# Sliding-window attention and an ELU layer on one core: first loads reordered, two score steps moved, the last step split

## The chip, the core and the metric

The kernel runs on one core of one Trainium2 chip, in one launch. The metric is the device time of that core in microseconds (us), lower is better. Before the change it is 311.78 us, the median of 8 runs (311.09 to 313.75). One run was taken with the hardware profiler; every line quoted from a page, a timeline or a DMA view is from such an execution.

## The reference

q, k and v are fp32 of shape (8 batches, 8 heads, 576 tokens, 64). The attention looks 32 tokens to each side; its result, with the heads side by side, is the input of a two-layer block with an ELU between the layers.

```python
scores = (q @ k.T) / sqrt(64)             # per batch and head
scores = where(|i - j| <= 32, scores, -1e9)
attn   = exp(scores - max) ; attn /= sum + 1e-9
x      = (attn @ v) as (4608 tokens, 512)
h      = x @ w_in                          # (512, 2048)
g      = where(h > 0, h, exp(min(h, 0)) - 1)
out    = g @ w_out                         # (2048, 512) -> (4608, 512) fp32
```

## The kernel before, in words

**Attention by pairs.** The 576 tokens of a batch are 9 query blocks of 64; two blocks make a pair, and there are 36 pairs. For a pair, `scores` (L279, PE, 16 matmuls) multiplies 128 keys by 64 queries per head into two PSUM banks, `exponential` (L290, ACT) writes them to SBUF, `mask` (L299, DVE) zeroes what lies outside the window, `pv` (L311, PE, 16 matmuls) multiplies by the values with a column of ones, `normalize` (L320 and L323, DVE) divides, `x_transpose` (L332, PE) turns the result and `x_evac` (L345, a copy on the engine named) puts it into `xT`. `V_e` holds the values in tiles of 128 tokens that start 32 tokens early; `V_o` is the same shifted by 64, made by `rotate_v` (L136, DVE) from two neighbouring tiles. `edges(i)` clears the borders of value buffer i and sets its ones.

**q and k.** `load_qk` (L115) loads one half of the tokens of a batch (`HALF_A`: tokens 0 to 287, `HALF_B`: 288 to 575) or all, in two transfers of 288 KB for the two heads of each couple (576 KB for all the tokens). `cast_qk` makes bf16 of them, `transpose_qk` (L262, PE) transposes, and a copy on ACT or DVE puts the result into `qT` or `kT`. Pairs 0 and 1 need only the first half of batch 0, pairs 2 and 3 its second half. Values and weights are loaded by POOL (L129, L150, L157) with a cast to bf16, on one queue in the order of issue; `load_w_in(c)` and `load_w_out(c)` bring a quarter each ("slice c"), enough for two of the eight steps of a tile. SP and ACT have queues of their own (q1 and q10 in the profile; POOL's is q0).

**The two layers by steps.** A tile t is 256 tokens, two pairs; there are 18. A step is a tile and a group s of 256 of the 2048 hidden units, so 144 steps in all. `mm1(kk)` (L540, 8 matmuls) makes the first product of step kk in one PSUM bank (tags h0 and h1 in turn), then ACT takes the exponential (L546) and DVE subtracts one (L548); `elu(kk)` (L553, DVE) takes max and min; `mm2(kk)` (L568, 4 matmuls) adds the second product into the two banks `psY` of the tile. Tiles 0 and 1 take turns: steps 0 to 3 are tile 0 with slices 0 and 1, steps 4 to 7 tile 1 with the same slices, so the values of pairs 2 and 3 are needed from step 4 on. When a tile is complete its two banks are copied to SBUF and written by SP; in the last tile each bank is copied in halves, by ACT and DVE, and written from the ACT and SP queues.

**What sets the order.** The schedule is written out by hand: each engine executes in program order, and a tile's dependencies add the waits. Before the loop there is a front (L376 to L407): casts, transposes, scores and the rest of pairs 0 and 1, with `idle(n, tag)` matmuls on zeros (L370) between them. In the loop (L591) the slots of step kk come in the order "first", `elu(kk-1)`, "dve", `mm1(kk)`, "mid", `mm2`, "end", and `at(kk, slot, ...)` puts work into one. A table gives the `mm2` of the first steps: `{1: (0,), 2: (1,), 3: (2,), 4: ()}`; after it, `mm2(kk-2)` belongs to step kk. A `gate` (L143) is a transfer of one element: it makes SP wait until what it reads is there, and so holds what SP issues behind it. One waits for `w_out` slice 0, and behind it stand batch 1's first q and k loads.

Of the kernel before, what the change touches and what calls it, by code (L numbers as in the profile page):

```python
# [9 lines left out]
FP32 = mybir.dt.float32  # L10
BF16 = mybir.dt.bfloat16
# [10 lines left out]
def kernel(  # L22
# [9 lines left out]
    nc = tc.nc  # L32
# [81 lines left out]

    def load_qk(b, which, part, eng=nc.sync):  # L115
        z, nj = part
        t = lpool.tile([128, 2, nj * D], FP32, tag=f"f{which}{nj}",
                       name=f"f{which}")
        qk_f[b, which, z] = t
        src = (q, k)[which][b, :, z * NC * nj:(z + 1) * NC * nj, :].rearrange(  # L120
            "(g h) (c j) d -> c g h (j d)", h=2, j=nj)
        for h in range(2):
            eng.dma_start(out=t[:, h, :], in_=src[:, :, h, :])

    def load_v(b, m):
# [5 lines left out]
            in_=v[b, :, lo + p0:lo + p1, :].rearrange("h p d -> p h d"))  # L131

    def rotate_v(b, m0, m1, parts=(0, 1)):
        e, o = V_e[b % 3], V_o[b % 3]
        for z in parts:
            nc.vector.tensor_copy(o[64 * z:64 * (z + 1), m0:m1],  # L136
                                  e[64 * (1 - z):64 * (2 - z),
                                    m0 + z:m1 + z])

    gate_t = cpool.tile([1, 8], BF16, name="gate_t")  # L140
    gates = [0]

    def gate(src):  # L143
        n = gates[0]
        gates[0] += 1
        nc.sync.dma_start(out=gate_t[:, n:n + 1], in_=src)

# [16 lines left out]

    for part in (HALF_A, HALF_B):
        load_qk(0, 0, part)
        load_qk(0, 1, part, nc.scalar)

# [3 lines left out]
    def edges(i):  # L172
# [22 lines left out]
        out=masks, in_=masks, compare_op=ALU.is_ge, fill=0.0,  # L195
        base=2 * WIN, pattern=[[0, 5], [1, QB]], channel_multiplier=-1)
    for mi in (0, 4):
        nc.gpsimd.affine_select(
            out=masks[:, mi, :], in_=masks[:, mi, :], compare_op=ALU.is_ge,
            fill=0.0, base=-WIN, pattern=[[0, QB]], channel_multiplier=1)  # L200
# [5 lines left out]

    for m in (1, 0, 2, 3, 4):
        load_v(0, m)
# [166 lines left out]

    idle(10, "y1")  # L376
    front_cast(0, HALF_A, nc.vector)
    front_transpose(0, HALF_A, nc.scalar, ("h0", "h1"))
    idle(2, "u")
    front_cast(1, HALF_A, nc.vector)  # L380
    for (j0, n), tag, eng in zip(SPLIT, ("y0", "y1"), (nc.scalar, nc.vector)):
        transpose_qk(0, 1, HALF_A, j0, n, eng, tag)
    for i, tag in ((0, "s"), (1, "u")):
        scores(i, tag)
        exponential(i)
    idle(2, "y0")
    front_cast(0, HALF_B, nc.vector)
    front_transpose(0, HALF_B, nc.scalar, ("h0", "h1"))
    mask(0)
    cast_qk(0, 1, HALF_B, *SPLIT[0], nc.vector)  # L390
    mask(1)
    cast_qk(0, 1, HALF_B, *SPLIT[1], nc.vector)
    idle(6, "y1")
    front_transpose(1, HALF_B, nc.scalar, ("y0", "y1"))
    rotate_v(0, 0, 2)
    for i in (0, 1):
        pv(i)
    for i in (0, 1):
        normalize(i)
    edges(2)  # L400
    rotate_v(0, 2, VS - 1)
    idle(4, "h0")
    for i in (0, 1):
        x_transpose(i)
    for i in (0, 1):
        x_evac(i, nc.scalar)
    idle(5, "h1")  # L407

    gate(w_out_sb[0:1, NFO // 4 - 1, D_MODEL - 1:D_MODEL])
    for which in range(2):  # L410
        load_qk(1, which, HALF_A)
    for c in range(2, 4):
        load_w_in(c)
        load_w_out(c)
        if c == 2:
            for m in range(3):
                load_v(1, m)
    gate(w_in_at(3))
# [28 lines left out]
    for i, tag in ((2, "s"), (3, "u")):  # L447
        at(0, "mid", scores, i, tag)
        at(0, "mid", exponential, i)
        at(1, "dve", mask, i)  # L450
        at(1, "end", pv, i)
        at(2, "dve", normalize, i)
        at(3, "mid", x_transpose, i)
    at(3, "mid", x_evac, 2, nc.scalar)
    at(3, "mid", x_evac, 3, nc.vector)
    at(4, "dve", swap_pools)

    for part, kq in ((HALF_A, 7), (HALF_B, 15)):
        for which in range(2):
            at(kq - 1 + which, "mid", cast_qk, 1, which, part, 0, SJ // 2,  # L460
               (nc.scalar, nc.vector)[which])
            at(kq + which, "mid", transpose_qk, 1, which, part, 0, SJ // 2,
               nc.scalar, "s")
    for m in range(VS):
        at(16 + m, "mid", load_v, 2, m)
# [66 lines left out]
    def mm1(kk):  # L532
        t, s = order[kk]
        h = kk % 2
        ps = ps_tile([128, FG, TT], FP32, f"h{h}", "ps")
        psH[kk] = ps
        for j in range(FG):
            fo = s * FG + j
            for do in range(NDO):
                nc.tensor.matmul(  # L540
                    ps[:, j, :],
                    lhsT=w_in_sb[:, do, fo * 128:(fo + 1) * 128],
                    rhs=xT[t][:, :, do, :],
                    start=(do == 0), stop=(do == NDO - 1))
        e_sb = mpool.tile([128, FG, TT], FP32, tag="e_sb")
        nc.scalar.activation(e_sb, ps, AX.Exp)  # L546
        m_sb = mpool.tile([128, FG, TT], BF16, tag="m_sb")
        nc.vector.tensor_scalar(m_sb, e_sb, -1.0, None, ALU.add)  # L548
        m_t[kk] = m_sb

    def elu(kk):
        g_sb = mpool.tile([128, FG, TT], BF16, tag="g_sb")
        nc.vector.scalar_tensor_tensor(  # L553
            g_sb, psH.pop(kk), 0.0, m_t.pop(kk), ALU.max, ALU.min)
        g_t[kk] = g_sb

    out_t = out.rearrange("(t ts p) c -> t p ts c", p=128, ts=TT // 128)

    def mm2(kk):
# [6 lines left out]
        for ts in range(2):  # L566
            for j in range(FG):
# [5 lines left out]
                    stop=(s == STEPS - 1 and j == FG - 1))  # L573
            if last:

                half = D_MODEL // 2
                for c, eng in enumerate((nc.scalar, nc.vector)):
                    y_sb = opool.tile([128, half], FP32, tag=f"y_last{c}",
                                      name="y_last")
                    copy_on(eng, y_sb, psY[t][ts][:, c * half:(c + 1) * half])  # L580
                    (nc.scalar, nc.sync)[c].dma_start(
                        out_t[t, :, ts, c * half:(c + 1) * half], y_sb)
        if s == STEPS - 1 and not last:
            for ts, eng in enumerate((nc.scalar, nc.vector)):
                y_sb = opool.tile([128, D_MODEL], FP32, tag=f"y_sb{ts}",
                                  name="y_sb")
                copy_on(eng, y_sb, psY[t][ts])
                nc.sync.dma_start(out_t[t, :, ts, :], y_sb)

    LAG = 2  # L590
    for kk in range(NSTEP + LAG):  # L591
        run(kk, "first")
        if 1 <= kk <= NSTEP:
            elu(kk - 1)
# [4 lines left out]

        for n in {1: (0,), 2: (1,), 3: (2,), 4: ()}.get(  # L600
                kk, (kk - LAG,) if kk >= LAG else ()):
            mm2(n)
# [31 lines left out]
```

The softmax here doesn't subtract the row's maximum and nothing guards it: scores larger than these inputs give would overflow.

## Time and profile before

| | |
|---|---|
| median of 8 runs | 311.78 us |
| the profiled execution's own time | 311.12 us |
| its span in the trace | 309.4 us |
| PE, DVE, ACT, POOL busy | 293.5, 247.0, 169.9, 43.1 us |
| step 0's first product starts | 18.15 us |
| last first product (step 143) ends, by the chain | 301.9 us |
| last matmul ends | 304.9 us |
| read from and written to HBM | 36.70 MB, 15.34 MB |

A timeline line has: start and duration in us, the engine, the line of the kernel, the operation, what it writes "<-" what it reads, the shape, and how many instructions were merged (x8); in brackets stands how long the engine was idle before and what ended that. PEld is PE's weight load, SPq and ACTq the instructions that issue transfers. A DMA view's queue line has packets, MB written and the share of the 16 DMA engines. The granted TensorE clock of the whole span is 0.995.

### The profile page before, as it was taken

Reading aid. Unit: us, or ns where it says so; the run is one execution under the profiler, and the core shown is the slowest. Engines: PE = TensorE matmul, PEld = TensorE weight load, DVE = VectorE, ACT = ScalarE, POOL = GpSimd, SP = SyncE. Lnnn points to the kernel's source line nnn. Section 1 sums busy time; section 2 is a strip of 40 time slices with the busy share of each in tenths; the row PEclk is TensorE's granted clock in tenths of the full one; section 3 lists DMA queues with packets and bytes.
Section 4 is the critical chain, followed back from the end, with each engine's and each line's share of the span. In section 5 each row is a group of like instructions: output and inputs, shape, how many; then the busy total and the mean of one; then the engine's idle time right before and its main releaser. Section 6 shows DMA issues by size and latency. Waiting matters only on the chain.

```text
span 309.4 us, 7519 instructions
## 1 busy us (share of the span) xinstructions
PE 293.5 (95%) x3003; PEld 197.2 (64%) x3057; DVE 247.0 (80%) x479; ACT 169.9 (55%) x255; POOL 43.1 (14%) x60
## 2 busy tenths in 40 slices
PE   6789998999999999999999999999999999999993
PEld 2456666577665666666666666666666666666661
DVE  5787687899979788888888888888888787877663
ACT  2753755777664674667366736663535354543431
POOL 8632542040111202020202000000000000000000
PEclk9999999999999999999999999999999999999998
DMA  6999999999979899599999999388111111111012
GB/s 240 193 207 270 189 162 364 373 229 289 245 171 196 309 244 197 148 154 255 240 159 202 301 238 196 110 166 169 70 36 70 34 70 35 70 34 70 24 46 69
DMA packets 91943, 52.93 MB, mean 171 GB/s; under 512 B 76548, under 2 KB 81156, under 8 KB 91908
## 3 DMA queue, kind: packets, MB, share of 16 engines
q1 hardware_dynamic: 47876, 36.19, 45.6%
q0 software_dynamic: 41728, 8.92, 39.0%
q10 hardware_dynamic: 2304, 7.34, 7.0%
q8 instruction: 24, 0.39, 0.5%
q14 instruction: 11, 0.09, 0.1%
HBM read 36.70 MB, written 15.34 MB: 168 GB/s over the span
## 4 chain that ended last, share of the span: by engine, by line
PE 76%; DVE 11%; DMA 6%; issue 3%; ACT 3%; ACTq 0%; SPq 0%; DVEq 0%
PE ps L540 35%; PE psY L568 33%; DMA Ve<-in_v_dram 5%; PE psS L311 3%; DVE g_sb L553 3%; PE psS L279 3%; DVE m_sb L548 2%; DVE pm L299 2%; PE ptx L262 1%; DMA f<-in_q_dram 1%; DVE x_st L323 1%; DVE Vo L136 1%; ACT e_sb L546 1%; DVE qkb L225 1%; ACT pu L290 1%
## 5 line engine op out<-in xcount | busy, mean ns | idle before, releaser
L546 ACT ACTIVATE e_sb<-ps 128x512 f32<-128x512 f32 x144 | 86.1, 598 | 121.9 <-PE ps L540 115.4
L540 PE MATMUL ps<-xT,w_in_sb 128*128 128x256 bf16 x1152 | 149.3, 273 | 1.0 <-DVE g_sb L553 0.8
L568 PE MATMUL psY<-w_out_sb,g_sb 128*128 128x512 bf16 x524 | 139.4, 379 | 3.8 <-issue 0.6
L540 PEld LDWEIGHTS <-w_in_sb 128*128 128x128 bf16 x1152 | 110.6, 98 | 39.6 <-issue 1.3
L553 DVE SCALAR_TENSOR_TENSOR g_sb<-ps,m_sb 128x512 bf16<-128x512 f32 x144 | 99.3, 689 | 12.4
L548 DVE TENSOR_SCALAR m_sb<-e_sb 128x512 bf16<-128x512 f32 x144 | 62.2, 432 | 36.4 <-ACT e_sb L546 34.4
L568 PEld LDWEIGHTS <-g_sb 128*128 128x128 bf16 x576 | 54.4, 98 | 39.5 <-DVE g_sb L553 1.7
L129 POOL DMA_DIRECT2D Ve<-in_v_dram x40 | 34.6, 871 | 128.3 <-PE psS L311 95.9
L290 ACT ACTIVATE pu<-psS 128x1024 bf16<-128x1024 f32 x36 | 36.5, 1019 | 1.4 <-PE psS L279 1.4
L323 DVE TENSOR_TENSOR x_st<-psS,rc 128x512 bf16<-128x512 f32 x36 | 24.9, 692 | 1.2
L223 ACT CAST qkb<-f 128x768 bf16<-128x768 f32 (+1 forms) x30 | 25.4, 848 | 0.0
L299 DVE TENSOR_TENSOR pm<-pu,masks 128x1024 bf16<-128x1024 bf16 x36 | 24.6, 682 | 0.7 <-ACT pu L290 0.7
L311 PEld LDWEIGHTS <-pm 128*64 128x64 bf16 x576 | 11.1, 110 | 10.3 <-DVE pm L299 6.6
L136 DVE COPY Vo<-Ve 64x1040 bf16<-64x1040 bf16 x32 | 14.2, 445 | 1.0
L311 PE MATMUL psS<-Ve,pm 128*64 128x65 bf16 x320 | 13.5, 196 | 0.1
L311 PE MATMUL psS<-Vo,pm 128*64 128x65 bf16 x256 | 12.1, 196 | 1.6 <-DVE pm L299 0.8
L279 PEld LDWEIGHTS <-kT 64*128 64x128 bf16 x576 | 9.5, 95 | 5.3 <-issue 4.2
L279 PE MATMUL psS<-qT,kT 64*128 64x64 bf16 x576 | 11.9, 191 | 0.9 <-DVE kT L225 0.9
L225 DVE COPY y_sb<-psY 128x512 f32<-128x512 f32 x17 | 11.6, 685 | 0.8 <-PE psY L568 0.8
L225 DVE CAST qkb<-f 128x1152 bf16<-128x1152 f32 (+3 forms) x16 | 10.3, 665 | 1.7 <-DMA f<-in_q_dram 1.7
L370 PE MATMUL ps_idle<-zeros 128*128 128x512 bf16 x27 | 9.1, 473 | 1.3 <-DVE zeros L170 1.3
L262 PE MATMUL ptx<-ident,qkb 128*128 128x128 bf16 x108 | 8.5, 220 | 1.8 <-DVE qkb L225 1.4
(33 smaller groups left out, 69.9 us busy)
## 6 DMA issues: line engine op xcount, KB each, us to landing
out_dram<-y_sb SPq DMA_DIRECT2D x34, 256.0 KB, 3.0
f<-in_q_dram SPq DMA_DIRECT2D x12, 576.0 KB, 9.2
f<-in_k_dram SPq DMA_DIRECT2D x12, 576.0 KB, 10.5
in_dram<-qkb ACTq DMA_DIRECT2D x10, 576.0 KB, 7.2
Ve<-in_v_dram POOLq DMA_DIRECT2D x24, 128.0 KB, 10.9
f<-in_q_dram SPq DMA_DIRECT2D x8, 288.0 KB, 7.3
w_in_sb<-in_moe_w_in_dram POOLq DMA_DIRECT2D x4, 512.0 KB, 15.8
w_out_sb<-in_moe_w_out_dram POOLq DMA_DIRECT2D x4, 512.0 KB, 16.2
```

What stands on the lines that cost most here:

```text
L129: nc.gpsimd.dma_start(out=V_e[b % 3][p0:p1, m, :, 0:D], in_=v[b, :, lo + p0:lo + p1, :].rearrange("h p d -> p h d"))
L223: nc.scalar.copy(d_, s_)
L279: nc.tensor.matmul(psS[:, h % 2, hp * 128 + z * QB:hp * 128 + (z + 1) * QB], lhsT=kT[b % 2][base:base + 64, KPAD + hp * S + QB * qb - WIN: ...
L290: nc.scalar.activation(pu, _bap(psS, [psS.ap[0], [1, 1024]]), AX.Exp, scale=SCALE)
L299: nc.vector.tensor_mul(pm, pu, _bap(mm, [mm.ap[0], [0, H], [1, 2 * QB]]))
L311: nc.tensor.matmul(psS[QB * z:QB * (z + 1), par, hp * VD:(hp + 1) * VD], lhsT=pm[:, par * HP + hp, z * QB:(z + 1) * QB], rhs=vv[:, qb // 2 ...
L323: nc.vector.tensor_mul(x_st, _bap(psS, [psS.ap[0], [VD, HP], [512, 2], [1, D]]), _bap(rc, [rc.ap[0], [2, HP], [1, 2], [0, D]]))
L540: nc.tensor.matmul(ps[:, j, :], lhsT=w_in_sb[:, do, fo * 128:(fo + 1) * 128], rhs=xT[t][:, :, do, :], start=(do == 0), stop=(do == NDO - 1))
L546: nc.scalar.activation(e_sb, ps, AX.Exp)
L548: nc.vector.tensor_scalar(m_sb, e_sb, -1.0, None, ALU.add)
L553: nc.vector.scalar_tensor_tensor(g_sb, psH.pop(kk), 0.0, m_t.pop(kk), ALU.max, ALU.min)
L568: nc.tensor.matmul(psY[t][ts], lhsT=g_sb[:, j, ts * 128:(ts + 1) * 128], rhs=w_out_sb[:, s * FG + j, :], start=(s == 0 and j == 0), stop=( ...
```

## The change

- **First loads.** Of batch 0's first half, q and k are each loaded by SP (one half of the heads) and ACT (the other). Values 1, 0, 2 are issued on POOL ahead of the last three selects that make the masks. A gate on a finished mask then holds SP, and behind it the second half of q and k is loaded, by SP alone.
- **Later loads.** Batch 1's first half of q and k waits for the second half of batch 0's q, not for `w_out` slice 0. POOL waits for the second half of k before `w_in` slice 2.
- **Front.** The second half's casts (q on ACT, k on DVE), transposes and copies come after the normalization of pairs 0 and 1, `rotate_v(0, 0, 2)` comes ahead of their masks. The idle matmuls are 8, 1, 1, 4, 2, 1, 1, 4 (before: 10, 2, 2, 6, 4, 5).
- **Steps 0 to 4.** Scores and exponentials of pairs 2 and 3 (the third and fourth) go from step 0 to step 1; their masks, products and normalization to the "dve" slot of step 2, with `mm2(1)` after the masks; `mm2(2)` goes from step 3 to step 4.
- **Values of batch 2.** `edges(2)` moves into step 8; `hold_v(2)`, a memset in step 16, must be done before batch 2's first value tile can be loaded.
- **Tail.** In step 143 the first product is made in two banks ("h1" and "s") of one hidden group of 128 each, each with its own exponential, subtraction and ELU. The last two banks of the output are copied whole, the first by DVE, the second by ACT, and written from SP and ACT.

The diff, cut to its core:

```diff
-    def load_qk(b, which, part, eng=nc.sync):
+    def load_qk(b, which, part, engs=(nc.sync, nc.sync)):
...
-            eng.dma_start(out=t[:, h, :], in_=src[:, :, h, :])
+            engs[h].dma_start(out=t[:, h, :], in_=src[:, :, h, :])
...
+    def hold_v(b):
+        nc.vector.memset(V_e[b % 3][64:65, :, 0, 0:1], 0.0)
...
-    def gate(src):
-        n = gates[0]
+    def gate(src, dt=BF16, eng=nc.sync):
         gates[0] += 1
-        nc.sync.dma_start(out=gate_t[:, n:n + 1], in_=src)
+        t = cpool.tile([1, 1], dt, name=f"gate{gates[0]}")
+        eng.dma_start(out=t, in_=src)
...
-    for part in (HALF_A, HALF_B):
-        load_qk(0, 0, part)
-        load_qk(0, 1, part, nc.scalar)
+    for which in range(2):
+        load_qk(0, which, HALF_A, (nc.sync, nc.scalar))
...
+    for m in (1, 0, 2):
+        load_v(0, m)
     for mi in (0, 4):
         nc.gpsimd.affine_select(
...
-    for m in (1, 0, 2, 3, 4):
+    gate(masks[0:1, 3, 0:1])
+    for which in range(2):
+        load_qk(0, which, HALF_B)
+    for m in (3, 4):
         load_v(0, m)
...
-    idle(10, "y1")
+    idle(8, "y1")
...
-    idle(2, "y0")
-    front_cast(0, HALF_B, nc.vector)
-    front_transpose(0, HALF_B, nc.scalar, ("h0", "h1"))
-    mask(0)
-    cast_qk(0, 1, HALF_B, *SPLIT[0], nc.vector)
-    mask(1)
-    cast_qk(0, 1, HALF_B, *SPLIT[1], nc.vector)
-    idle(6, "y1")
-    front_transpose(1, HALF_B, nc.scalar, ("y0", "y1"))
+    idle(4, "y0")
     rotate_v(0, 0, 2)
     for i in (0, 1):
-        pv(i)
+        mask(i)
+    pv(0)
+    idle(2, "h0")
+    pv(1)
     for i in (0, 1):
         normalize(i)
-    edges(2)
+    front_cast(0, HALF_B, nc.scalar)
+    idle(1, "h1")
+    x_transpose(0)
+    x_evac(0, nc.scalar)
+    for (j0, n), tag in zip(SPLIT, ("y0", "y1")):
+        transpose_qk(0, 0, HALF_B, j0, n, nc.scalar, tag)
+    x_transpose(1)
+    x_evac(1, nc.scalar)
+    front_cast(1, HALF_B, nc.vector)
+    idle(1, "h0")
+    for (j0, n), tag, eng in zip(SPLIT, ("s", "u"), (nc.vector, nc.scalar)):
+        transpose_qk(0, 1, HALF_B, j0, n, eng, tag)
     rotate_v(0, 2, VS - 1)
-    idle(4, "h0")
-    for i in (0, 1):
-        x_transpose(i)
-    for i in (0, 1):
-        x_evac(i, nc.scalar)
-    idle(5, "h1")
-
-    gate(w_out_sb[0:1, NFO // 4 - 1, D_MODEL - 1:D_MODEL])
+    idle(4, "h1")
+
+    gate(qk_f[0, 0, 1][0:1, 1, 0:1], FP32)
     for which in range(2):
         load_qk(1, which, HALF_A)
+    gate(qk_f[0, 1, 1][0:1, 1, 0:1], FP32, nc.gpsimd)
...
     for i, tag in ((2, "s"), (3, "u")):
-        at(0, "mid", scores, i, tag)
-        at(0, "mid", exponential, i)
-        at(1, "dve", mask, i)
-        at(1, "end", pv, i)
+        at(1, "mid", scores, i, tag)
+        at(1, "mid", exponential, i)
+        at(2, "dve", mask, i)
+    at(2, "dve", lambda: mm2(1))
+    for i in (2, 3):
+        at(2, "dve", pv, i)
         at(2, "dve", normalize, i)
-        at(3, "mid", x_transpose, i)
-    at(3, "mid", x_evac, 2, nc.scalar)
-    at(3, "mid", x_evac, 3, nc.vector)
+        at(3, "mid" if i == 3 else "dve", x_transpose, i)
+        at(3, "mid" if i == 3 else "dve", x_evac, i, nc.scalar)
...
+    at(8, "dve", edges, 2)
+    at(16, "dve", hold_v, 2)
...
+        tags = (f"h{h}", "s") if kk == NSTEP - 1 else (f"h{h}",)
+        w = FG // len(tags)
...
+            if kk == NSTEP - 1:
+                elu(kk, z)
...
+            for ts in range(2):
+                z = 1 - ts if last else ts
+                eng = (nc.scalar, nc.vector)[z]
...
                 copy_on(eng, y_sb, psY[t][ts])
-                nc.sync.dma_start(out_t[t, :, ts, :], y_sb)
+                (nc.scalar if last and ts else nc.sync).dma_start(
+                    out_t[t, :, ts, :], y_sb)
...
-        if 1 <= kk <= NSTEP:
+        if 1 <= kk < NSTEP:
             elu(kk - 1)
...
-        for n in {1: (0,), 2: (1,), 3: (2,), 4: ()}.get(
+        for n in {1: (0,), 2: (), 3: ()}.get(
```

## The prediction, made before the changed kernel was built or run

> **What bounds the kernel now.** I read the page first: PE is busy for 95% of the span, and the chain of work that ended last is 76% PE. In the timeline a loop step is 0.87 us of the first product (8 matmuls of L540) and 0.86 us of the second (4 of L568), nearly back to back from about 30 us to 302 us. The change removes no PE work there; what it can move is the start, the tail and a few gaps. So the timeline of 0 to 32 us came next:
>
> ```profile
> 18.15 1.04 PE L540 MATMUL ps<-xT,w_in_sb 128*128 128x256 bf16 x8
> ...
> 21.15 1.04 PE L568 MATMUL psY<-w_out_sb,g_sb 128*128 128x512 bf16 x3 [0.41 <-DVE g_sb L553]
> ...
> 23.04 1.05 PE L540 MATMUL ps<-xT,w_in_sb 128*128 128x256 bf16 x8 [0.16 <-DMA w_in_sb<-in_moe_w_in_dram]
> ...
> 30.30 1.03 PE L540 MATMUL ps<-xT,w_in_sb 128*128 128x256 bf16 x8 [0.20 <-DVE g_sb L553]
> ```
>
> Step 0 starts at 18.15. The row at 30.30 is step 6, with pairs 2 and 3 and the second product of steps 0 to 3 done: that moment is my yardstick for the start, and what moves it moves the end. Step 2, at 23.04, waits for a weight slice, so the start runs close to the pace of the transfers. The tile views (issue plus time to landing) put w_in 0 at 8.0+8.9 = 16.9, w_out 0 at 8.7+11.7 = 20.4, w_in 1 at 23.0 and w_out 1 at 25.5. What the transfers can do is in the DMA view of single stretches, 16 to 20 us, 27 to 30 us and 48 to 58 us (queue, packets, MB):
>
> ```profile
> q0 software_dynamic: 815, 0.81, 122.7%
> ```
> ```profile
> q1 hardware_dynamic: 285, 0.59, 58.0%
> q0 software_dynamic: 286, 0.28, 55.4%
> ```
> ```profile
> q1 hardware_dynamic: 959, 3.57, 95.4%
> q0 software_dynamic: 958, 0.12, 18.3%
> ```
>
> q0 casts fp32 to bf16, so it reads twice what it writes. Weights alone read 2x0.81/4 = 0.41 MB/us; beside q and k loads, 2x0.28/3 = 0.19 next to 0.20; q and k beside values move 0.36 while values get 0.012. Every mix reads about 0.4 MB/us. Values alone (10 to 13 us) write 148 GB/s, so read 0.3.
>
> The tail comes last: the timeline from 302 us.
>
> ```profile
> 301.93 1.67 PE L568 MATMUL psY<-w_out_sb,g_sb 128*128 128x512 bf16 x7
> ...
> 303.83 1.04 PE L568 MATMUL psY<-w_out_sb,g_sb 128*128 128x512 bf16 x4 [0.22 <-DVE g_sb L553]
> 304.47 0.37 ACT L223 COPY y_last<-psY 128x256 f32<-128x256 f32 x1 [1.95 <-PE psY L568]
> ...
> 304.87 0.42 DVE L225 COPY y_last<-psY 128x256 f32<-128x256 f32 x1 [1.10 <-ACT y_last L223]
> ...
> 305.68 0.42 DVE L225 COPY y_last<-psY 128x256 f32<-128x256 f32 x1 [0.38 <-ACT y_last L223]
> ```
>
> The half copies of one bank run one after the other, DVE behind ACT, and the last transfer is issued at 306.1.
>
> **The change, part by part.**
>
> *Tail.* PE has the second products of steps 141 and 142 until 301.93+1.67 = 303.60, so splitting the ELU can win only the wait of 0.22. The halves' price is by the nearest rows: exp 0.37 (ACT, 128x256), DVE 0.27 (half of 0.43, plus some fixed cost) and 0.42. DVE is free of the previous ELU at 302.03; 2x(0.27+0.42) and 0.2 of gaps end at 303.6, just in time. At full price for each half it would be some 0.1 late instead. The first bank is complete 0.64 after the start: 304.25, DVE copies it whole (0.69) until 304.94; the second at 304.65, ACT copies it (0.58) until 305.25, and its queue issues at 305.3, against 306.13. Landing took 2.3 for 128 KB; the 256 KB rows of the step before took 2.1, in pairs up to 2.6. The end moves from 308.4 to 307.4 to 307.9: **-0.8** (-0.5 to -1.0).
>
> *First loads.* The first half of q is split over SP and ACT. ACT's queue moved no data before 3 us (SP's did from 2 us), so q is whole at about 5.3, not 5.7; k stays at 6.4, as both queues carry the same 1.18 MB by 6. Worth 0.4 on the casts. The second half now waits on SP for the masks. On POOL three V issues (2.7 us, 0.9 each) are put ahead of the last selects, so the masks end at 3.48+2.70 = 6.2; the gate costs SP 0.87 (20.49 to 21.36), so the second half is issued from 7.1 instead of 2.15, first data 1.4 later at 8.5 (SP's very first load: issued at 0.81, data from 2.2). Behind the gate on SP are only loads. The values lose the backlog before them: first data when the first halves drain, near 6, and V 0 to 2 landed by about 10 instead of 13.1. That pulls rotation, masks and the products of pairs 0 and 1 forward by up to 2.5 us.
>
> How fast does the second half then come? The Trainium skill, "DMA: Bandwidth & Descriptors", section "Queues, rings and completion order", says that an engine takes turns between its queues packet by packet. Equal shares would give it 0.2 MB/us against the values: 5.9 us, k landing near 15. The row of 48 to 58 us gives it 0.36: 3.3 us, q landing near 10.7 and k near 12.4. I take the row. Casts, transposes and evacuations of both halves now stand before step 0 on ACT and DVE (q's casts 1.3 on ACT, four evacuations of 0.75), ending near 16.5; by the rule, near 18.5.
>
> *Batch 1's first half* now follows q's second half (gate at about 10.7, issued from 11.6) instead of w_out 0 (issued at 21.36, data near 25). It is 1.18 MB. Before, what had to be read for w_out 0 was 1.18 for each half of q and k, 1.18 of values and two slices of 1.05: 5.64 MB. Now up to 1.18 more comes ahead of it: by the 0.4 MB/us that every mix gives, 0 to 2.9 us. It shares evenly with the weights once it runs (27 to 30 us), from somewhere in 13 to 15.4, and some 0.7 of it passes before w_out 0 is through: +2.1, so w_out 0 lands at 22.5 (20.4 to 23.3). This is the step I trust most as to sign: no bandwidth is idle there to hide it. POOL's own gate (on k) holds only w_in 2, which the queue reaches later anyway: 0.
>
> *Order of steps 0 to 4.* Per step: exp 0.60, add 0.43, ELU 0.69. Without any weight wait, step 0's ELU is done 3.0 us after its start; the second products of steps 0 and 1 follow; then PE runs pair 2's product (0.45), waits 1.1 for its normalization (0.20+0.69 and gaps), transposes it (0.40), does pair 3's (0.45), and only then step 2. With 0.7 more for pair 3's evacuation before step 4, step 6 comes 13.9 after step 0, against 30.30-18.15 = 12.15 now: 1.75 of new waiting. From the second product of step 0 on it is 0.86+0.86+0.45+1.1+0.40+0.45 to step 2, and 0.87+0.87+0.40+0.70+0.87+0.86+0.87+0.86 to step 6, together 10.4. If w_out 0 lands at 22.5, step 6 comes at 32.9: **+2.6**. w_in 1 near 25 is in time for step 2 at 26.6.
>
> *Idle matmuls*, 10 down to 8 at the start. They are at half rate there: 10 in 4.45 us, while later 6 take 1.46. The page shows the clock as granted from the first slice, so by it this costs 0. The skill's "TensorE: Matmul & The Clock Gate", Part 1, says that full rate follows a busy free-running window of 3.4 us; 8x0.43 just fills that. By the rule the transposes of q and k and the first scores could run at half rate until the next window, up to +1.0. I take 0: it would fall before 22.5, under the wait for w_out 0.
>
> *edges(2)* (0.09+0.49+0.49 on DVE) moves to step 8, where DVE is busy for 64% (30 to 40 us): 0, at most +0.4. *hold_v(2)*, one tiny memset, makes POOL wait for step 16 (about 53 us) with V of batch 2 and all values behind it. They then miss the free stretch of 34 to 44 us and come when q and k loads end near 64; their rotation is at step 22 (69 us). Bounds -0.5 (batch 1's second half comes 1.5 us earlier; PE's gaps of 44 to 52 us sum to 1.0) to +1.0; I take 0.
>
> **Sum**, on the profiled execution's 311.12 us (span 309.40 and 1.72 around it): +2.6-0.8 = +1.8, 312.9. Its time is 0.66 below the median of 311.78; on the median, **313.6**.
>
> **Rivals.**
> 1. *Batch 1's load takes less* (it arrives late behind the weights, as at 21.36, when data took 3.7 us to start). Then w_out 0 stays near 20.4 and step 6 is at T+13.9 with T = 16.5 to 17.5: 30.4 to 31.4. Start +0.1 to +1.1, tail -0.8: 311.1 to 312.1. Chance 0.20, no change. For it: the late start of that load. Against: the queue is already running when it comes.
> 2. *Faster, through the values.* V 0 to 2 by 10 us set the pace of pairs 0 and 1, and overlapping values with the second half saves the quarter of bandwidth that values alone leave (1.18/0.3-1.18/0.4 = 1.0 us). Then w_in 0 lands at 15.9 and w_out 0 below 19.3; step 0 starts at 15.6 to 16, step 6 at 29.6, so -0.7, with the tail and a little from the gaps -1.7: 310.1. It decides if w_out 0 lands before 19.3 and step 0 starts before 16.2. Chance 0.18. Against it: 1.18 MB more in the same stretch.
> 3. *Worse: the second half lands late and the clock stays low.* k after 16.5 puts step 0 at 19 or later, step 6 at 33 to 34: 314 to 315.4. Chance 0.12.
> The main case has 0.50 (312.8 to 314.6).
>
> Faster or slower by over 0.3% (0.93 us, about what a measurement can tell from no change): slower is the main case and rival 3, 0.62; within, rival 1, 0.20; faster, rival 2, 0.18. The range, 310.6 to 315.4, leaves out part of rival 2 and the far end of rival 3. The slower cases alone: 312.8 to 315.4.
>
> **What would show it.** Right: in the changed timeline the first L568 waits for w_out and starts at 22 or later, q and k loads of batch 1 run between 12 and 22 us, PE waits for x_st between pairs 2 and 3, step 6 is near 33, and the last y_sb is issued near 305.3 after step 143's end as now. Wrong: w_out 0 landed by 20, or step 6 at 30 or before, or the last products waiting for the second half of the ELU.

## The result and the profile after

The changed kernel takes 314.86 us (median of 11 runs, 313.31 to 317.3); the kernel before, timed beside it, 311.68 us (32 runs, 310.79 to 313.75). The ratio is 1.0105, 95% interval 1.0085 to 1.0125: slower by 1.05%, or 3.2 us. The forecast was 313.6 us, slower.

The profiled execution of the changed kernel has an own time of 316.09 us and a span of 314.4. That is 1.23 above its median, while before's 311.12 lies 0.56 below the 311.68: of the 4.97 us between the two traces, 1.8 is chance of the two executions. Where the starts of the first products stand in both:

| first product of step | before, us | after, us | later by |
|---|---|---|---|
| 0 | 18.15 | 21.87 | 3.72 |
| 2 | 23.04 | 28.88 | 5.84 |
| 6 | 30.30 | 35.72 | 5.42 |
| 14 | 48.22 | 53.01 | 4.79 |
| 20 | 62.66 | 68.22 | 5.56 |
| 143 | 300.84 | 306.63 | 5.79 |
| end of the span | 309.40 | 314.40 | 5.00 |

All of the loss is there by step 2; from step 24 to step 143 the distance stays within 0.1 us; the tail gives 0.79 back. The page's chain keeps PE's share (75%, before 76%) and has 3% of the work of POOL in it, and its clock row has dips to 0.7 and 0.6 in the second and third slice, where before's (the last line) had none.

```profile
PEclk9769999999999999999999999999999999999999
...
PE 75%; DMA 12%; DVE 5%; POOL 3%; issue 2%; SPq 2%; ACT 1%; DVEq 0%; POOLq 0%
```
```profile
PEclk9999999999999999999999999999999999999998
```

The timeline from 16 to 38 us answers to the one of 0 to 32 us shown of before:

```profile
18.67 0.83 DVE L234 CAST qkb<-f 128x640 bf16<-128x640 f32 x2 [4.45 <-DMA f<-in_k_dram]
19.22 1.14 PE L271 MATMUL ptx<-ident,qkb 128*128 128x128 bf16 x9 [3.39 <-DVE qkb L234]
...
20.16 1.91 PE L379 MATMUL ps_idle<-zeros 128*128 128x512 bf16 x4
...
21.87 3.39 PE L562 MATMUL ps<-xT,w_in_sb 128*128 128x256 bf16 x16
...
25.76 1.04 PE L596 MATMUL psY<-w_out_sb,g_sb 128*128 128x512 bf16 x3
...
28.88 1.05 PE L562 MATMUL ps<-xT,w_in_sb 128*128 128x256 bf16 x8
...
35.72 1.04 PE L562 MATMUL ps<-xT,w_in_sb 128*128 128x256 bf16 x8
```

In the kernel before, the last transposes of k's second half and the last idle matmuls had run here:

```profile
13.23 0.40 PE L262 MATMUL ptx<-ident,qkb 128*128 128x128 bf16 x4 [0.32 <-DVE qkb L225]
...
17.07 1.24 PE L370 MATMUL ps_idle<-zeros 128*128 128x512 bf16 x5
```

What to see: `w_in` 0 landed at 18.4 and `w_out` 0 at 22.6 (issue at 8.98 plus 13.6), yet step 0 starts at 21.87 and the first L596 at 25.76, with no bracket: neither was waited for. DVE stood idle for 4.45 us for the second half of k, whose last transfer landed at 18.65 (issued at 9.1). PE stood for 3.39 behind that cast, and four idle matmuls and then the 16 matmuls of steps 0 and 1 ran at half rate: 16 in 3.39 us, where 8 take 0.87 in the loop. Windows of 3.4 us of the same kernel show how the clock went (stretch, length, busy time of PE, PEld, DVE, ACT, POOL with counts, granted clock, DMA share, GB/s):

```profile
7.80:11.20 3.40, 2.71 (x39) 1.71 (x41) 1.77 (x4) 1.81 (x3) 3.40 (x5) 0.50 1.47 169
11.20:14.60 3.40, 2.61 (x41) 1.10 (x39) 2.80 (x6) 1.30 (x3) 0.14 (x1) 1.00 1.23 237
14.60:18.00 3.40, 1.07 (x13) 0.79 (x14) 0.00 (x0) 2.74 (x6) 0.00 (x0) 1.00 1.19 254
18.00:21.40 3.40, 2.18 (x12) 1.40 (x13) 2.22 (x4) 0.72 (x1) 2.13 (x4) 0.51 1.15 280
21.40:24.80 3.40, 3.40 (x16) 2.28 (x15) 1.27 (x3) 0.60 (x1) 2.45 (x3) 0.50 1.15 283
```

PE had 1.07 us of work while it waited for k, and the next two windows ran at half rate, over step 0 and step 1. The DMA view of 9 to 17 us (queue, packets, MB written, share) shows why k came late:

```profile
q0 software_dynamic: 2155, 0.76, 80.9%
q1 hardware_dynamic: 572, 1.17, 49.1%
```

q1 is the second half of q and k, q0 reads twice its 0.76 MB: the two read 1.17 and 1.52 MB in 8 us, not far from even in bytes, though far from it in packets, and 0.34 MB/us in all. In shorter stretches q1 wrote 0.30 MB in 2 us both beside 1085 packets of q0 (0.14 MB, from 9 to 11 us) and beside 242 (0.25 MB, from 13 to 15).

The tail, the timeline from 302 us:

```profile
307.72 2.54 PE L596 MATMUL psY<-w_out_sb,g_sb 128*128 128x512 bf16 x11
...
308.85 0.42 DVE L581 SCALAR_TENSOR_TENSOR g_sb<-ps,m_sb 128x256 bf16<-128x256 f32 x1
...
309.86 0.69 DVE L234 COPY y_sb<-psY 128x512 f32<-128x512 f32 x1 [0.58 <-PE psY L596]
310.29 0.59 ACT L232 COPY y_sb<-psY 128x512 f32<-128x512 f32 x1 [2.21 <-PE psY L596]
310.58 0.33 SPq L609 DMA_DIRECT2D out_dram<-y_sb  x1
310.91 0.36 ACTq L609 DMA_DIRECT2D out_dram<-y_sb  x1
```

The two banks are copied whole and side by side, and the last transfer is issued 4.28 us after step 143's start; before it was 306.13-300.84 = 5.29.

**Two theories.** By the prediction, `w_out` 0 (and the weights behind it) comes late because batch 1's first half of q and k is read ahead of it. By the rival, named third in the prediction, the second half of batch 0 lands late, its casts and transposes then stand on the path, and the clock falls while PE waits. The trace of after speaks for the rival; but it shows only which wait was longer, not what is left when it is gone.

### The profile page after: what moved, and what is told of

Read it like the earlier page. It is cut to its first block, busy times and chain, and to the rows that moved or that the text cites. A ratio compares the mean times of both kernels' runs of the same rounds, so it can differ in the third digit from the quotient of the medians.

```text
span 314.4 us, 7516 instructions
## 1 busy us (share of the span) xinstructions
PE 295.5 (94%) x2997; PEld 198.4 (63%) x3050; DVE 247.6 (79%) x479; ACT 170.9 (54%) x257; POOL 43.8 (14%) x61
## 4 chain that ended last, share of the span: by engine, by line
PE 75%; DMA 12%; DVE 5%; POOL 3%; issue 2%; SPq 2%; ACT 1%; DVEq 0%; POOLq 0%
PE ps L562 34%; PE psY L596 33%; DMA w_out_sb<-in_moe_w_out_dram 6%; DMA Ve<-in_v_dram 4%; PE psS L320 3%; PE psS L288 3%; DMA f<-in_q_dram 2%; SPq L123 2%; POOL Ve L129 1%; DVE g_sb L581 1%; PE ptx L271 1%; DVE Vo L140 1%; DVE x_st L332 1%; DVE y_sb L234 1%; DVE pm L308 1%
## 5 line engine op out<-in xcount | busy, mean ns | idle before, releaser
L569 ACT ACTIVATE e_sb<-ps 128x512 f32<-128x512 f32 (+1 forms) x145 | 86.2, 595 | 122.5 <-PE ps L562 117.5
L596 PE MATMUL psY<-w_out_sb,g_sb 128*128 128x512 bf16 x525 | 139.2, 379 | 3.5 <-issue 0.6
L581 DVE SCALAR_TENSOR_TENSOR g_sb<-ps,m_sb 128x512 bf16<-128x512 f32 (+1 forms) x145 | 99.5, 686 | 13.0 <-PE ps L562 0.5
L571 DVE TENSOR_SCALAR m_sb<-e_sb 128x512 bf16<-128x512 f32 (+1 forms) x145 | 62.5, 431 | 35.8 <-ACT e_sb L569 33.7
L596 PEld LDWEIGHTS <-g_sb 128*128 128x128 bf16 x576 | 54.5, 98 | 39.0 <-DVE g_sb L581 1.1
L232 ACT CAST qkb<-f 128x768 bf16<-128x768 f32 (+3 forms) x32 | 26.7, 837 | 2.1 <-DMA f<-in_q_dram 2.1
L140 DVE COPY Vo<-Ve 64x1040 bf16<-64x1040 bf16 x32 | 15.0, 470 | 1.1
L320 PE MATMUL psS<-Ve,pm 128*64 128x65 bf16 x320 | 13.6, 196 | 0.1
L234 DVE COPY y_sb<-psY 128x512 f32<-128x512 f32 x18 | 12.3, 686 | 1.2 <-PE psY L596 1.2
L234 DVE CAST qkb<-f 128x1152 bf16<-128x1152 f32 (+3 forms) x14 | 8.7, 644 | 5.3 <-DMA f<-in_k_dram 4.8
L271 PEld LDWEIGHTS <-qkb 128*128 128x128 bf16 x108 | 7.0, 102 | 8.8 <-DVE qkb L234 6.6
```

The lines of the kernel that those rows point to most:

```text
L232: nc.scalar.copy(d_, s_)
L320: nc.tensor.matmul(psS[QB * z:QB * (z + 1), par, hp * VD:(hp + 1) * VD], lhsT=pm[:, par * HP + hp, z * QB:(z + 1) * QB], rhs=vv[:, qb // 2 ...
L581: nc.vector.scalar_tensor_tensor(g_t[kk][:, z * w:(z + 1) * w, :], ps, 0.0, m_t[kk][z], ALU.max, ALU.min)
L596: nc.tensor.matmul(psY[t][ts], lhsT=g_sb[:, j, ts * 128:(ts + 1) * 128], rhs=w_out_sb[:, s * FG + j, :], start=(s == 0 and j == 0), stop=( ...
```

## The experiments

Every ratio is to the kernel before, in runs on the same chip; n is the number of timed runs of the kernel tried.

**1. Batch 1's load back behind `w_out` 0.** In the changed kernel:

```diff
-    gate(qk_f[0, 0, 1][0:1, 1, 0:1], FP32)
+    gate(w_out_sb[0:1, NFO // 4 - 1, D_MODEL - 1:D_MODEL])
```

> The changed kernel with one gate put back: batch 1's first half of q and k waits for w_out slice 0 again, as before the change. Weights theory (the prediction's main step): the early 1.18 MB is what delays the start, so w_out 0 lands 2 us earlier and the time falls by about 2, to 312.8. Late-half theory (what the trace of the changed kernel suggests): step 0 waits for the second half of k, landed at 18.65, and batch 1's transfers move no data before 18; so w_out 0 lands 2 us earlier and nobody has waited for it: within 0.5 of the changed kernel's 314.9, at most a little less through w_in 1.

Measured: 314.9 us (n = 4), ratio 1.0097 [1.0067, 1.0128]. `w_out` 0 landed at 20.9 instead of 22.6 and `w_in` 1 at 23.45 instead of 26.7, but step 0 started at 21.76, step 2 at 28.69, step 6 at 35.47: 0.1 to 0.25 earlier than in after. The ratio is 0.08% below after's, not told apart from it. As the change stands, nobody waits for those slices. The rival holds here.

**2. The pause filled.** In the changed kernel the four idle matmuls that stand between the second half's transposes and step 0 are taken out, and eight are put where PE waits for k:

```diff
     front_cast(1, HALF_B, nc.vector)
-    idle(1, "h0")
+    idle(9, "h0")
...
     rotate_v(0, 2, VS - 1)
-    idle(4, "h1")
```

> The changed kernel with 9 idle matmuls instead of 1 ahead of the transposes of k's second half, and the last 4 idle matmuls taken out. The loads are untouched. It measures the clock's part: in the changed kernel's profile TensorE ran at half rate from 18.05 to 24.87, because nothing ran while it waited for k. If the late half and the clock share the loss, step 0 starts near 20 (1.7 earlier, the four matmuls at half rate), steps 0 and 1 take 0.87 each instead of 1.7, and the time falls by 2 to 3, to 312 to 313, with less spread between runs. If the clock has no part, only the idle matmuls are saved: 1 or less.

Measured: 313.95 us (n = 9), ratio 1.0063 [1.0041, 1.0085], 0.42% less than after. That is 0.9 us, which by the text above would mean that the clock has no part. The profile says otherwise: the matmuls run at full rate from about 13.2 us on, through the filled pause too (first line below), and step 0 starts at 18.97. But the timeline from 18 to 32 us now shows the prediction's waits:

```profile
14.60:18.00 3.40, 3.11 (x25) 1.75 (x27) 1.23 (x3) 2.83 (x6) 0.17 (x1) 1.00 1.19 246
```
```profile
18.97 1.92 PE L561 MATMUL ps<-xT,w_in_sb 128*128 128x256 bf16 x16 [0.46 <-DMA w_in_sb<-in_moe_w_in_dram]
...
23.12 1.89 PE L595 MATMUL psY<-w_out_sb,g_sb 128*128 128x512 bf16 x7 [1.66 <-DMA w_out_sb<-in_moe_w_out_dram]
...
26.95 1.05 PE L561 MATMUL ps<-xT,w_in_sb 128*128 128x256 bf16 x8 [1.30 <-DMA w_in_sb<-in_moe_w_in_dram]
```

PE comes 2.9 us earlier to step 0. Not all of that is the edit's doing as far as is known: k's last transfer landed at 17.2, 1.4 before after's 18.65, with the same loads issued at the same time. Then PE waits 1.66 us for `w_out` 0, which now lands at 23.08, and 1.30 for `w_in` 1 (26.9). Step 6 is at 33.73, 2.0 earlier than in after. So the two theories are two limits one behind the other, and this kernel stands at the second.

**3. Both at once:** experiment 2 with the gate of experiment 1.

```diff
-    gate(qk_f[0, 0, 1][0:1, 1, 0:1], FP32)
+    gate(w_out_sb[0:1, NFO // 4 - 1, D_MODEL - 1:D_MODEL])
```

> wait_filled with batch 1's first half of q and k gated on w_out slice 0, as before the change. In wait_filled step 0 started at 18.97 with the clock at full rate, but step 2 waited until 26.95 for w_in slice 1, landed at 26.9. Weights theory, now as the second limit that stands behind the late half: w_out 0 lands near 20.9 and w_in 1 near 23.5 (as in batch1_later), step 2 starts 5.7 after step 0 at about 24.7 and step 6 near 31.4: 2.3 less than wait_filled, 311.7. If batch 1's early load costs nothing here either, as in batch1_later, it stays at 313.9.

Measured: 311.91 us (n = 12), ratio 0.9997 [0.9972, 1.0022]. Its timeline:

```profile
15.70 1.89 PE L379 MATMUL ps_idle<-zeros 128*128 128x512 bf16 x8
...
17.30 0.83 DVE L234 CAST qkb<-f 128x640 bf16<-128x640 f32 x2 [2.11 <-DMA f<-in_k_dram]
...
18.57 1.92 PE L561 MATMUL ps<-xT,w_in_sb 128*128 128x256 bf16 x16
...
21.84 2.17 PE L595 MATMUL psY<-w_out_sb,g_sb 128*128 128x512 bf16 x7 [0.78 <-DVE g_sb L580]
```

The wait for `w_out` 0 is gone (landed at 20.9), that for `w_in` 1 too (23.5, step 2 at 24.58), and step 6 starts at 31.36. The same edit, the later load of batch 1, that was worth 1.0105-1.0097 = 0.08% in experiment 1 is worth 1.0063-0.9997 = 0.66% here, 2.0 us.

**4. What the filling is worth by itself.** Experiment 1 with one line taken out, and nothing put in:

```diff
     rotate_v(0, 2, VS - 1)
-    idle(4, "h1")
```

> filled_later without its filling: batch 1's first half gated on w_out 0, the last 4 idle matmuls gone, but only 1 idle matmul ahead of the transposes of k's second half. It parts the two edits of wait_filled. If the filling (the clock) is what helped, step 0 again runs at half rate and the time is 1 to 2 over filled_later's 311.9, at 313 to 314. If taking out the 4 matmuls in front of step 0 was what helped (1.7 at half rate), it is within 0.4 of 311.9.

Measured: 313.56 us (n = 12), ratio 1.0042 [1.0016, 1.0069]. In its profiled execution the clock fell again:

```profile
13.20:16.60 3.40, 1.64 (x18) 0.96 (x18) 0.70 (x2) 3.20 (x6) 0.00 (x0) 1.00 1.16 278
16.60:20.00 3.40, 1.03 (x10) 1.03 (x11) 1.11 (x3) 0.23 (x1) 0.99 (x2) 0.50 1.24 205
20.00:23.40 3.40, 3.40 (x18) 2.17 (x15) 2.83 (x5) 1.32 (x2) 3.40 (x5) 0.50 1.24 206
```

and its timeline has steps 0 and 1 at half rate:

```profile
18.42 0.83 DVE L234 CAST qkb<-f 128x640 bf16<-128x640 f32 x2 [4.49 <-DMA f<-in_k_dram]
...
18.97 1.14 PE L271 MATMUL ptx<-ident,qkb 128*128 128x128 bf16 x9 [3.43 <-DVE qkb L234]
...
19.90 3.62 PE L561 MATMUL ps<-xT,w_in_sb 128*128 128x256 bf16 x16
```

From experiment 1 to this one 0.55% went (step 2 from 28.69 to 27.15): that is the four idle matmuls, 1.91 us long in after's timeline, standing at half rate ahead of step 0. From this one to experiment 3 another 0.45%, 1.4 us, and the only edit between them is the filling. What the filling changes can be read from the two traces, where step 2 starts 2.57 us apart (27.15 and 24.58): 1.12 because the cast of k's last transfer starts later (18.42 and 17.30), and 1.45 behind that, at half clock (0.21 to step 0, 1.24 from there to step 2). In all three traces without the filling (after, experiments 1 and 4) k's last transfer landed at 18.4 to 18.65, in both with it (experiments 2 and 3) at 17.2; the loads are the same, the last few packets of q1 come later, and why is not shown. So the filling is worth 1.4 us, and the clock is a part of it, not shown to be all. In the two of its runs whose mean granted clock was 1.0 this kernel took 310.96 and 311.28 us, in the others 312.19 to 314.75. That mean can miss early half rate, though: experiment 7's profiled execution has 0.998 and 313.61 us, with matmuls at half rate until about 20.

**5. The first loads as before.** Experiment 1 with all eight loads of batch 0 issued at once, values after the masks, no gate on a mask; the front keeps the change's order.

```diff
-    for which in range(2):
-        load_qk(0, which, HALF_A, (nc.sync, nc.scalar))
+    for part in (HALF_A, HALF_B):
+        load_qk(0, 0, part)
+        load_qk(0, 1, part, (nc.scalar, nc.scalar))
...
-    for m in (1, 0, 2):
-        load_v(0, m)
...
-    gate(masks[0:1, 3, 0:1])
-    for which in range(2):
-        load_qk(0, which, HALF_B)
-    for m in (3, 4):
+    for m in (1, 0, 2, 3, 4):
         load_v(0, m)
```

> As batch1_later, and with batch 0's second half loaded as before the change: all eight loads of q and k at once from SP and ACT, the five value loads behind the masks, no gate on a mask. The order of the work on the engines stays the changed kernel's. Late-half theory: k's second half lands near 10 instead of 18.65, step 0 starts near 18 or when w_in 0 lands near 17, the TensorE clock does not fall back before step 0, and the time is 3 or more below batch1_later: 311 to 312. Weights theory: the bytes ahead of w_out 0 are the same, so w_out 0 lands where batch1_later has it, and the time is within 0.5 of that kernel.

Measured: 314.01 us (n = 7), ratio 1.0067 [1.0044, 1.0091]: a miss. k's second half landed at 10.0, but values 0 to 2 at 13.3, and the changed front puts the second half's casts and transposes after pairs 0 and 1, which need those values. So nearly all of that work came after 13.3, at half clock until 18.3, and step 0 at 21.23. The order of the front and the order of the loads belong together: with the old loads the new front makes step 0 late. (The new loads with the old front were not run.)

**6 and 7. Without the gate on the mask.** First on top of experiment 3, then on top of experiment 4; the second half of q and k is issued at once, by SP alone.

```diff
-    gate(masks[0:1, 3, 0:1])
```

> filled_later without the gate on a mask: SP loads batch 0's second half right behind the first, the values keep their place ahead of the last selects. Late-half theory in its plain form: the second half lands near 10 instead of 12 to 17.3, step 0 is no longer held by k and starts when w_in 0 is there, near 17: 0.5 to 1.5 less than filled_later, 310.5 to 311.4. If instead the values are then pushed behind the second half (landing near 13, as before the change) and pairs 0 and 1 wait for them with all of the second half's work still to follow on ACT and DVE, step 0 stays at 18.5 or later: 311.9 or more.

> later_unfilled without the gate on a mask; so no_mask_gate without the 9 idle matmuls, which stood in its way (2.1 us of them, 18.20 to 20.30, while k's second half had been there since 11.0). Step 0 follows pairs 0 and 1, whose values land near 13: step 0 near 18.7 at full clock, near 19.5 if the clock stays low, so 311.9 to 312.8. If the second half's earlier arrival were worth its 6 us, step 0 would start at w_in 0's landing near 17: 310.5 to 311.

Measured: 314.53 us (n = 4), ratio 1.0097 [1.007, 1.0124], and 312.88 us (n = 13), ratio 1.0024 [1.0, 1.0049]. The first is spoilt by its own filling, as its timeline shows:

```profile
12.50 0.88 DVE L140 COPY Vo<-Ve 64x1040 bf16<-64x1040 bf16 x2 [3.31 <-DMA Ve<-in_v_dram]
...
18.20 2.10 PE L378 MATMUL ps_idle<-zeros 128*128 128x512 bf16 x9
```

k landed at 11.0, so PE no longer waited for it; it waited for the values (12.9), and the nine idle matmuls ended at 20.3, ahead of step 0 at 20.64. Without the filling the interval overlaps that of experiment 4 (1.0042): taking the gate away trades k at 18.4 (values at 9.5) for values at 13.5 (k at 11.8), and no gain or loss is shown. Why k took 9.5 us from its issue is therefore read from the DMA view alone.

**8. The tail alone.** The kernel before with the change's `mm1`, `elu` and last copies, of which these lines are the core:

```diff
-        ps = ps_tile([128, FG, TT], FP32, f"h{h}", "ps")
+        tags = (f"h{h}", "s") if kk == NSTEP - 1 else (f"h{h}",)
...
-            if last:
...
+                z = 1 - ts if last else ts
+                eng = (nc.scalar, nc.vector)[z]
```

> The kernel before with the tail of the change alone (step 143's first product in two banks, the last two banks copied whole). Both theories of the start expect the same here: the last product follows its predecessors without the gap of 0.22 us, the last transfer is issued 0.8 us earlier, and the whole is 0.8 us (0.5 to 1.0) under the kernel before, near 310.9. The trace of the changed kernel fits that: from the end of step 143's first product to the end of the span it has 0.8 less. If the tail is worth nothing, the time stays at 311.7.

Measured: 310.89 us (n = 22), ratio 0.9977 [0.996, 0.9995]. The last transfer is issued at 305.39, 4.27 after step 143's start, as in after.

**9. Eight idle matmuls instead of ten.** The kernel before with one edit:

```diff
-    idle(10, "y1")
+    idle(8, "y1")
```

> The kernel before with 8 idle matmuls instead of 10 at the start, nothing else. If the 3.4 us of 8 matmuls are too short for a busy window, the half-rate time shows in the profile after the first full window, and the time rises by 0.5 to 2, with a wider spread between runs. If the loss of clock in the changed kernel comes only from the later waits, nothing changes: within 0.3 of 311.8.

Measured: 312.6 us (n = 12), ratio 1.0017 [0.9996, 1.0038]; not told apart from 1. In its profiled execution matmuls ran at half rate until about 13.9, step 0 started at 19.55, step 6 at 31.63 (1.33 late), and 0.81 was left from step 14 on.

**10. The order of steps 0 to 4.** The kernel before with the change's `at` lines for pairs 2 and 3 and its `mm2` table:

```diff
-        at(0, "mid", scores, i, tag)
-        at(0, "mid", exponential, i)
-        at(1, "dve", mask, i)
-        at(1, "end", pv, i)
+        at(1, "mid", scores, i, tag)
+        at(1, "mid", exponential, i)
+        at(2, "dve", mask, i)
+    at(2, "dve", lambda: mm2(1))
...
+        at(3, "mid" if i == 3 else "dve", x_transpose, i)
...
-        for n in {1: (0,), 2: (1,), 3: (2,), 4: ()}.get(
+        for n in {1: (0,), 2: (), 3: ()}.get(
```

> The kernel before with the new order of steps 0 to 4 alone (scores of pairs 2 and 3 in step 1, second product of step 1 in step 2, of step 2 in step 4). The prediction priced the order at 1.75 of new waiting: step 6 at 32.0, time 313.5. The profiles of the changed kernel and of loads_back show only 12.5 from step 0 to step 6 at full clock, against 12.15: step 6 at 30.6, 0.2 to 0.5 more than before.

Measured: 312.3 us (n = 12), ratio 1.0005 [0.9983, 1.0028]. Step 6 starts 12.5 us after step 0 (31.81-19.31); before it was 12.15. (Step 0 itself came 1.16 late in this execution, at half clock from 7.7 to 14.5; the edit begins behind it.)

**11. The values of batch 2.** The kernel before with `edges(2)` in step 8 and `hold_v(2)` in step 16:

```diff
-    edges(2)
...
+    at(8, "dve", edges, 2)
+    at(16, "dve", hold_v, 2)
```

> The kernel before with the memsets of value buffer 2 moved into step 8 and batch 2's value loads held until step 16. In the changed kernel's profile steps 13 to 14 gained 0.65 and steps 19 to 21 lost 0.9. If that is the hold (POOL issues its value loads in one stretch, and DVE's copies take up to twice as long beside them, once at 44 to 48 us before, now near 60), the same gain and loss show here: +0.2, within 0.5 of before. If the gain came from batch 1's earlier loads instead, only the loss is left: +0.9.

Measured: 312.36 us (n = 21, without one of 316.59), ratio 1.0014 [0.9995, 1.0033]; not told apart from 1. Its trace shows a gain and a loss. At step 6 it is 0.81 us behind before (PE waited 0.88 for `w_in` 1 ahead of step 2), at step 14 only 0.17, as the copies of `V_o` at 45 us no longer meet POOL's issues: a gain of 0.64. By step 20 it has lost 0.35 again and by step 24 0.25 more. The first of these is paid at 61 us, where the copies now do meet the issues:

```profile
56.78 4.44 POOL L129 DMA_DIRECT2D Ve<-in_v_dram  x5
...
60.69 1.24 DVE L139 COPY Vo<-Ve 64x1040 bf16<-64x1040 bf16 x2
...
62.95 0.40 PE L335 MATMUL psXT<-ident,x_st 128*128 128x128 bf16 x4 [0.62 <-DVE x_st L326]
```

**12. What is worth keeping.** The kernel before with the tail of experiment 8, twelve idle matmuls at the start instead of ten, and two more ahead of the first scores:

```diff
-    idle(10, "y1")
+    idle(12, "y1")
...
+    idle(2, "h0")
     for i, tag in ((0, "s"), (1, "u")):
         scores(i, tag)
```

> A version meant to beat both: the kernel before with the tail of the change, 12 idle matmuls instead of 10 at the start and 2 more ahead of the first scores. Clock theory: profiles of the same front fell to half rate from 7.6 to 14.5 in one execution and not in another, so a fuller first 10 us makes the loss rarer: median 0.2 to 0.5 under tail_alone, near 310.5, with fewer runs above 312. If the clock's phase costs nothing in this front, the same as tail_alone, 310.9; if the extra matmuls stand in the way of the transposes, up to 0.5 more.

Measured: 310.51 us (n = 17, 309.71 to 311.1), ratio 0.9963 [0.9951, 0.9976]: the lowest median, better than both kernels. Against experiment 8 the intervals overlap, so a gain of the added idle matmuls over the tail is not shown. All 17 runs had a mean granted clock of 0.997 or more; of experiment 8's 22 runs, four had 0.986 to 0.989 and took 311.5 to 312.75, but its longest, 314.63, had 1.0.

## Why the prediction was right in sign and range, and where its steps failed

The sign held, and so did the range of 310.6 to 315.4; the main case did not. Its 312.8 to 314.6, with a chance of 0.50, leaves 314.86 out, and two of its signs are missing in after: the first L568 (now L596) does not wait for `w_out`, and PE does not wait for `x_st` between pairs 2 and 3. Step 6 came at 35.72, not near 33. What happened is rival 3, which had 0.12. So the closeness of 313.6 is in part luck: in the kernel as it stands the late weights, the main term, cost nothing that could be told from zero (experiment 1), and the late second half, which the sum had at nothing, stood in their place.

Along one chain of runs the +1.05% splits so:

| from, to | what it carries | change of the ratio |
|---|---|---|
| after, experiment 2 | late second half: idle matmuls on the path, half clock, k's own landing | 0.42% = 1.3 us |
| experiment 2, experiment 3 | batch 1's early load | 0.66% = 2.0 us |
| experiment 3, before with the tail | order of steps, values of batch 2, what is left of the start | 0.20% = 0.6 us |
| before with the tail, before | the tail | -0.23% = -0.7 us |

The links are differences of ratios with intervals of about 0.2 to 0.3% at each end; the third is not told apart from zero. The first two depend on their order. Taken the other way, by experiment 1, the early load is worth 0.08%, and the late second half behind it 1.0097-0.9997 = 1.00%, 3.1 us.

- **Tail, -0.8: right.** -0.7 by the medians, 0.79 by the traces.
- **`w_out` 0 at 22.5, +2.1: the size was right, its place was not.** It landed at 22.6 (20.9 in experiment 1), and where it is felt batch 1's load costs 2.0. Some 0.7 MB of that load did pass ahead of it (0.68 MB on q1 from 18 to 22 us), though from 18.4 on and not from 13 to 15.4. But in the kernel as it stands it was not the last to arrive: the sum held it against the step's data alone, and took the second half's casts and transposes as done by 16.5. In after k's transposes end at 20.36 (19.22 plus 1.14), and the four idle matmuls behind them hold PE until 21.87. Rival 3 named that mechanism. (Its step 6 at 33 to 34 comes to 313.7 to 314.7 by the sum's own rule, not to 314 to 315.4.)
- **"I take the row": the step that failed.** The row of 48 to 58 us gave k at 12.4, the equal shares that I drew from the Trainium skill, "DMA: Bandwidth & Descriptors", section "Queues, rings and completion order", near 15; it was 18.65. In 9 to 17 us the queues moved about even bytes, so the equal shares came nearer. They do not confirm the page's turns packet by packet, as q0 moved 2155 packets and q1 572. What their sum still lacked is the start (first data near 9.5, not 8.5), the rate (0.34 MB/us for both, not 0.4) and the end (nearly all data had moved by 17, single packets came until 18.2, landed at 18.65). The row was one of a stretch whose conditions I had not matched: there values alone stood on q0 behind a long backlog of q1; here the values and weights were in their queue before q1's second half was issued. That this is what made the difference is argued, not shown.
- **The clock, taken as 0: failed.** I looked only at the two idle matmuls removed at the start (experiment 9: 0.17%, not told apart from 0), and let any loss fall under the wait for `w_out` 0. The larger loss came from the new pause at 14.6 to 18 us, which no line of before shows. The rule of the Trainium skill, "TensorE: Matmul & The Clock Gate", Part 1, on busy and idle windows of 3.4 us fits the length of the windows above, but a window with 1.07 us of work already counted as idle here; put beside equal shares, which left PE without data until about 15, it would have asked for a price.
- **Idle matmuls of the change itself: left out of the sum.** The last four stand in front of step 0, and experiment 4 against experiment 1 gives them 0.55%, 1.7 us, of which the wait for the weights takes back a part when they go (experiment 2).
- **Order of steps, 1.75: failed.** Experiment 10 gives 0.05%, its trace 0.35 us. PE does not wait for pair 2's normalization before pair 3: `x_transpose(2)` stands in the slot of step 3, behind step 2's product, and runs at 29.76 in after, when its `x_st` was done (29.62). I had read it into step 2. (The terms that the prediction lists, 3.0 and 10.4, come to 13.4 from step 0 to step 6 and not to 13.9; 1.75 rests on the latter.) In experiment 2 the stretch from the second product of step 0 to step 6 is still 33.73-23.12 = 10.6, near the 10.4 of the sum, but for another reason: a wait of 1.30 for `w_in` 1, which I had put near 25 and which landed at 26.9.
- **Values of batch 2 and `edges(2)`, 0: right within what can be told** (0.14% [-0.05, 0.33]), as a gain of about 0.6 and a loss of about the same.

So the +2.6 of the start was, by the sum's own numbers, 1.35 for the weights (the first L568 at 22.5 instead of 21.15) and 1.25 for the order behind it (10.4 against 30.30-21.15 = 9.15). The runs give next to nothing for the order, and 3.3 us for the late second half and the weights together; how it divides depends on which is removed first.

Left open: how much of k's late landing is due to the gate's late issue (7.2 instead of 2.15) and how much to the shared engines; experiments 6 and 7 changed both. Why k landed 1.2 to 1.4 us earlier in the two traces with the filled pause, and what the split of the first loads over SP and ACT is worth by itself, no run shows. The granted clock could not be held fixed in the changed kernel, so the profiled executions show one course of it each, and the medians a mix.

## What to carry to other kernels

Before a late transfer is named as the bound, follow every other chain to the same instruction, with the casts, transposes and filler matmuls between a landing and its use: here two limits lay 3 us apart one behind the other, and the cure of the second was worth 0.08% until the first was gone and 0.66% after. When a reordering makes PE wait, price the clock as well as the wait, and put filler where PE waits, so that it ends before the data land; in front of the first useful matmul it costs its own length, at half rate twice. The rate at which two queues share the engines is to be taken from a stretch with the same kinds of transfers on both, or kept as a range.

## What the runs showed of the hardware

**The clock moves in steps of 3.41 us**, whose phase differs from run to run: half from 7.81, full from 11.22, half from 18.05, full from 24.87 in after (3.41, 6.83 and 6.82 apart); half from 7.55 to 14.38 in experiment 3. A window with 1.07 us of work was followed by half rate, and one at half rate with 2.18 of 3.40 by another. In the filled pause of experiment 2 (3.11 of 3.4 busy from 14.6 to 18.0) it stayed full. Cut along these steps from 4 to 49 us, the traces of after and of experiments 1, 3, 4, 5, 6 and 10 have nine full-rate windows with 1.07 to 1.87 us of PE work, all followed by half rate, while those with 1.93 or more stayed at full rate; experiment 2 has one with 1.75 that stayed. Of the half-rate windows, those with 3.2 us or more were followed by full rate and those with 2.61 or less were not; from 2.71 to 2.77 both occur. Before the first clock record a profile shows 1.00 although idle matmuls run 0.43 us apart rather than 0.22: the clock row of before was read too kindly for its first microseconds.

**DVE's copies slow down beside POOL's issues of value loads.** Two copies of `V_o` take 0.88 us alone (at 49.61 in after) and 1.66 here:

```profile
60.52 7.78 POOL L129 DMA_DIRECT2D Ve<-in_v_dram  x9
...
65.31 1.66 DVE L140 COPY Vo<-Ve 64x1040 bf16<-64x1040 bf16 x2
...
67.99 0.40 PE L341 MATMUL psXT<-ident,x_st 128*128 128x128 bf16 x4 [1.05 <-DVE x_st L332]
```

PE then waits 1.05 us for `x_st`, where before it waited 0.27; the difference, 0.78, is close to the 0.76 that after loses between steps 19 and 20. A `TENSOR_SCALAR` of 0.43 took 0.87 at 45.52 in before, also beside such issues, while `x_st`, made from PSUM, keeps its 0.69. The Trainium skill, "SBUF — State Buffer", section "SBUF: two separate sides", has DVE and GpSimd share a pair of ports under an exclusive lock; the rows fit that, and no run here tries it by itself.
